# Linear attention and a top-2 expert layer on one core: 32-row gathers issued one at a time over two layers' loops, and a reordered start

## The chip, the cores and the metric

One core of a Trainium2 chip runs the whole kernel. The metric is device time in microseconds. The kernel before took 741.69 us (median of 3 runs, 741.14 to 741.85).

## The reference, cut to what matters

Inputs are q, k, v of shape (4, 8, 768, 64), a decay lam per head, gate and noise weights (512 x 8), noise (3072 x 8), and expert weights w1 (8, 512, 1024) and w2 (8, 1024, 512).

```python
for b in range(nb):                                   # linear attention, a state per head
    intra = einsum('bhij,bhjd->bhid', einsum('bhic,bhjc->bhij', qb, kb) * Dmask, vb)
    inter = einsum('bhid,bhde->bhie', qb * lam_pow, kv_state)
    kv_state = lam_block * kv_state + einsum('bhsd,bhse->bhde', kb * rev_pow, vb)
x = attention output as (3072 tokens, 512)
noisy = x @ w_gate + log1p(exp(x @ w_noise)) * noise  # the two best experts of a token
out[t] = sum over its two experts of weight * (relu(x[t] @ w1[e]) @ w2[e])
```

Dmask, lam_pow and rev_pow are powers of lam. Everything is float32.

## The kernel before, in words

**Attention.** Each of the 12 steps u takes 256 tokens (chunks of 128) of one batch, three steps to a batch. `trans_k` and `trans_q` (L315, L327) transpose k and q on TensorE into PSUM banks `pS` (four of them, taken in turn by `bank()`), evacuated by ScalarE (VectorE for step 0); `trans_q` also lets VectorE write `qTs`, q scaled by `QS`. `scores` (L353) multiplies q by k, and VectorE applies the mask `Mk` into `at`. `kdecay` (L344) scales k on GpSimd into `kd`, of which there is one buffer. `kv` (L401) multiplies kd by v, and `state` (L414) lets VectorE add that to the state. `intra` and `inter` (L381, L376) accumulate the output in the banks `pO` and `pKV`, `evac_o` copies it out, and a step later `store_x`, `products` and `logits` store x and form the gate logits.

**The masks.** VectorE builds the powers of lam by doubling in `pp2`. SyncE (SP) stores them to the DRAM tile `powd` (L203) and loads `at` (L206) and `QS` (L210) from it. VectorE turns `at` round into `Mk` (`make_mask`, L216). All loads of q, k, v, weights and gate weights `wgn` (L667) go through SP's queue in program order. Here `wgn` comes after the loads of step 2.

**The order.** The schedule is written out by hand: each engine works in program order, and waits follow from data and buffers. Before the loop: `trans_k(0)`, `trans_q(0)`, `scores(0)`, `kdecay(0)`, `kv(0)`, `state(0)`, `inter(0, 1)`. The loop of step t (L951) does, for u = t + 1, `trans_k(u)`, `trans_q(u)`, `kv(u)`, `state(u)`, `kdecay(t + 2)`, then `intra(t)`, `inter(t, 0)`, then `scores(u)` and the logits of t - 1. Routing (VectorE) is spread over the steps by `advance`.

**Experts.** For each expert e there is `gemm1` (16 calls, L857: two parts of at most 4 and 3 token tiles by 8 blocks f) and then `gemm2`, one call for each of 6 or 7 token tiles (L893), a tile's result going by VectorE (L919) into one of two `ot` buffers. GpSimd scatters `ot` to the output (`scatter_out`, L926) and fetches what the output held before (`gather_prev`, L891). Beside tile t of `gemm2(e)`, `trans_rows(e + 1, j)` (L829) transposes a tile of gathered rows of the next expert (VectorE, ScalarE), and `gather_rows(e + 2, j)` (L814) refills its buffer `xg`. For e >= 2 a tile is gathered as up to four pieces of 32 columns' width each (L819, an indirect DMA on GpSimd's queue). In the loop of expert 1 the pieces of expert 2, a tile at a time, stand beside the second part of `gemm1(1)` (L1197 to L1199), behind a small copy (`spacer`, L1195) that waits for that block's `ht`; those of expert 3 stand beside `gemm2(1)`.

Of the kernel before, what the change touches and what calls it, by code (L numbers as in the profile page):

```python
# [31 lines left out]
C = 128  # L32
# [5 lines left out]
E = 8  # L38
# [32 lines left out]
X1 = ((), (0,), (1,), (2,), (3,), (4,), (5, 6))  # L71
WARM = (14, 4, 4)
GB = (0, 8, 16, NCH)
# [52 lines left out]
def kernel(  # L126
# [16 lines left out]
    x_tok = dram.tile([NTOK, XW], FT, name="x_tok")  # L143
    powd = dram.tile([H, 2, 256], FT, name="powd")

# [36 lines left out]

    keep_warm(WARM[0])
    for nm in ("kt", "qt"):
        load(0, nm)
    jp = ac.tile([128, 128], I32, name="jp")
# [3 lines left out]
    pp2 = aw.tile([H, 2, 512], FT, name="kd", bufs=1)[:, :, :256]  # L190
    pw, pr = pp2[:, 0, :], pp2[:, 1, 0:255]
    nc.vector.memset(pp2[:, 1, 255:256], 0.0)
    sq = ac.tile([H, 8], FT, name="sq")
    nc.vector.memset(pw[:, :127], 0.0)
    nc.vector.memset(pw[:, 127:128], 1.0)
    nc.vector.tensor_copy(sq[:, 0:1], lamc)
    for i in range(7):
        n = 1 << i
        nc.vector.tensor_scalar(pw[:, 127 + n:127 + 2 * n], pw[:, 127:127 + n], sq[:, i:i + 1], None, op0=MULT)
        nc.vector.tensor_mul(sq[:, i + 1:i + 2], sq[:, i:i + 1], sq[:, i:i + 1])  # L200
    nc.vector.tensor_copy(pw[:, 255:256], sq[:, 7:8])
    nc.vector.tensor_copy(pr, pw[:, 254::-1][:, :255])
    nc.sync.dma_start(powd, pp2)  # L203
    mrev = aw.tile([128, H, C], FT, name="at")
    for a in range(2):
        nc.sync.dma_start(mrev[a * 64:(a + 1) * 64], sub(powd, 256, [[2, 64], [512, H], [1, C]]))  # L206
    load(0, "vt")
    QS = ac.tile([128, HP, C], FT, name="QS")
    for s in range(2):
        nc.sync.dma_start(QS[s * 64:(s + 1) * 64], sub(powd, 128 + 512 * s, [[0, 64], [1024, HP], [1, C]]))  # L210
    Mk = ac.tile([128, 2, HP, C + 1], FT, name="Mk")
    nc.gpsimd.memset(Mk[:, :, :, 0:1], 0.0)

    def make_mask():
        for s in range(2):
            nc.vector.tensor_copy(Mk[:, s, :, 1:], mrev[:, s:H:2, ::-1])  # L216

    def mask(s, h, c):

        m = Mk[:, s, h, c.start + 1:c.stop + 1]  # L220
        return sub(m, 0, [*m.ap[:2], [-1, 2], m.ap[2]])

    for nm in ("kt", "qt", "vt"):
        load(1, nm)
    wgn = ac.tile([128, DB, 32], FT, name="wgn")
    nc.gpsimd.memset(wgn[:, :, 2 * E:], 0.0)
# [36 lines left out]
    class Arena:  # L263
# [4 lines left out]
        def tile(self, shape, dt, name):  # L268
            n = math.prod(shape[1:])
            if name not in self.at:  # L270
                self.at[name], self.end = (self.end, n), self.end + n
            at, most = self.at[name]
            assert n <= most and self.end <= self.buf.shape[1], (name, self.end)
            __import__("sys").stderr.write(f"AR {self.end} ")
# [38 lines left out]

    def trans_k(u):

        kT[u] = aw.tile([128, HP, 2, C], FT, name="kT", bufs=1)
        flat = KT[u].rearrange("p h x d -> p (h x d)")
        for at, y, r in ((D, 1, slice(0, 128)), (0, 0, half(0)), (2 * D, 0, half(1))):
            p = bank()
# [7 lines left out]
    def trans_q(u, scaled=True):  # L327

        qT[u] = aw.tile([128, HP, 2 * C], FT, name="qT", bufs=1)
        qTs[u] = aw.tile([128, HP, 2 * C], FT, name="qTs")  # L330
        for a in range(2):
            p = bank()
# [34 lines left out]
    def add_out(u, a, hp, s, lhs, rhs):  # L367

        if u not in PO:
            PO[u] = [psum.tile([128, DB, C], FT, name=nm) for nm in ("pO", "pKV")]  # L370
            first[u] = {}
        g = side(s, hp)
        n = first[u][a, g] = first[u].get((a, g), 0) + 1
        nc.tensor.matmul(PO[u][a][half(g), hp, :], lhs, rhs, start=n == 1,  # L374
                         stop=n == (12 if u % NW or a else 8))

# [55 lines left out]
    XC = [ac.tile([128, DB, QW], FT, name=f"xc{i}") for i in range(3)]  # L432
    for x in XC:
        nc.gpsimd.memset(x[:, :, C:], 0.0)
    xturn = itertools.count()
# [211 lines left out]

    trans_k(0)
    trans_q(0, False)
    make_mask()  # L650
    keep_warm(WARM[1])
    scores(0)
    nc.vector.tensor_mul(qTs[0][:, :, C:], qT[0][:, :, C:], QS)
    kdecay(0)
    keep_warm(WARM[2])
    kv(0)
    state(0)
    make_sel()
    kdecay(1)
    load(2, "kt")  # L660
    load(2, "qt")
    load(2, "vt")
    inter(0, 1)
    for s, w in ((0, w_gate), (1, w_noise)):
        for d in range(2):
            for h in range(2):
                nc.sync.dma_start(wgn[h * 64:(h + 1) * 64, d::2, s * E:(s + 1) * E],  # L667
                                  sub(w, (d * 128 + (h ^ d) * 64) * E, [[E, 64], [256 * E, DB // 2], [1, E]]))

# [132 lines left out]
    def load_rec(e, queue=nc.sync):  # L802
# [7 lines left out]
        if e >= TURNED:  # L810
# [3 lines left out]
            RECQ[e] = r  # L814

    def gather_rows(e, t, rows=NTOK):
        if e >= TURNED:
            for g in range(size(e, t) // 32):
                nc.gpsimd.indirect_dma_start(  # L819
                    out=XG[t][:, g * QW:(g + 1) * QW], out_offset=None,  # L820
                    in_=x_tok.rearrange("t (q w) -> (t q) w", w=QW),
                    in_offset=bass.IndirectOffsetOnAxis(ap=RECQ[e][:, t, g:g + 1], axis=0),
                    bounds_check=4 * NTOK - 1, oob_is_err=False)
            return
# [123 lines left out]
    def early(b):  # L948

        return [(b, 2 * i, 2, x) for i, x in enumerate(HB[:4 if not b else 2])]  # L950

    got = []
    for t in range(NST):
        u = t + 1
        if u < NST:
            trans_k(u)
        load(t + 3, "kt")
        if u < NST:
            trans_q(u)
        load(t + 3, "qt")  # L960
        if u < NST:
            kv(u)
            state(u)
            kdecay(t + 2)
            if REC and not got:
                for j in range(PARTS0[0]):
                    gather_rows(0, j, GB[1] * C)
                got.append(t)
            advance(FILLS)
        else:  # L970
# [209 lines left out]
    for e in range(1, E):  # L1180
        if e == E - 1:
            n_over = nc.values_load(ntot[0:1, 0:1], min_val=0, max_val=MAXOV)
        if e == 1:
            prepare(2)
        for i, (t0, n) in enumerate(parts(e)):
            for f in range(FB):
# [17 lines left out]
        for t in range(tiles(e)):  # L1204
# [3 lines left out]
            if e + 1 < E:  # L1208
# [83 lines left out]
```

## Time and profile before

| | |
|---|---|
| median of 3 runs | 741.69 us |
| profiled execution | 743.33 us, span 741.5 us |
| TensorE (PE) busy | 706.8 us (95%) |
| VectorE (DVE) | 400.7 us (54%) |
| GpSimd (POOL) | 352.4 us (48%) |
| ScalarE (ACT) | 223.1 us (30%) |
| mean granted TensorE clock | 0.981 |

The profiled execution is one run; its span is from the first to the last instruction. Times in the rows are microseconds from the start of that span unless marked ns. Attention runs to about 145 us, expert 0 to 232 us, and experts 1 to 7 follow.

### The profile page before, as it was taken

The numbers are of one execution on the slowest core, as the hardware profiler recorded it, in microseconds if no ns is written. First come the engines' busy times: TensorE is split into PE (matmuls) and PEld (weight loads), VectorE is DVE, ScalarE is ACT, GpSimd is POOL, SyncE is SP. The second block draws the span as 40 slices with busy tenths as digits, with TensorE's granted clock in tenths as the row PEclk, the third lists the DMA queues.
The fourth block names the chain that finished last, engine by engine and source line by source line (L and its number), as shares of the span: only waits on it lengthen the run. The fifth ranks groups of instructions, "written<-read, shape, count | busy, mean of one in ns | idle before, by whom it ended". The sixth has DMA issues, their size and how long they took to land.

```text
span 741.5 us, 15923 instructions
## 1 busy us (share of the span) xinstructions
PE 706.8 (95%) x6014; PEld 606.1 (82%) x6014; DVE 400.7 (54%) x1053; ACT 223.1 (30%) x381; POOL 352.4 (48%) x503
## 2 busy tenths in 40 slices
PE   6999899999999996879999999999999999999994
PEld 4887788889898895678889887988898898889883
DVE  5645788879456543573457255626552763465210
ACT  0354456451133321132214221422142242214100
POOL 2312163214353488775378547845763776221221
PEclk9899999999999999889999999999999999999998
DMA  7899896681546624445245534634362546230211
GB/s 172 179 270 240 235 231 181 223 308 48 160 141 162 188 50 118 135 128 138 76 166 145 132 101 136 163 91 128 119 157 84 156 147 163 62 136 27 64 43 37
DMA packets 95608, 104.59 MB, mean 141 GB/s; under 512 B 42130, under 2 KB 68260, under 8 KB 95528
## 3 DMA queue, kind: packets, MB, share of 16 engines
q1 hardware_dynamic: 82232, 66.57, 33.9%
q0 software_dynamic: 13296, 36.97, 16.3%
q8 instruction: 49, 0.80, 0.4%
q14 instruction: 31, 0.25, 0.1%
HBM read 78.54 MB, written 26.13 MB: 141 GB/s over the span
## 4 chain that ended last, share of the span: by engine, by line
PE 82%; issue 6%; DMA 4%; DVE 3%; POOL 2%; ACT 1%; SPq 0%; POOLq 0%; DVEq 0%; ACTq 0%
PE pS L869 36%; PE pKV L907 14%; PE pO L907 13%; PE pS L362 3%; PE pO L374 2%; PE pS L321 2%; PE pKV L374 2%; PE pS L442 2%; DMA out_dram<-ot,rec 2%; PE pO L912 1%; PE pS L409 1%; PE pS L334 1%; POOL xg L819 1%; DMA QS<-powd 1%; PE pR L428 1%
## 5 line engine op out<-in xcount | busy, mean ns | idle before, releaser
L869 PE MATMUL pS<-xth,w1h 128*128 128x512 f32 (+3 forms) x544 | 182.5, 335 | 4.6 <-DVE ht L879 4.6
L819 POOL DMA_INDIRECT xg<-x_tok,recq x147 | 160.8, 1094 | 51.0 <-issue 26.6
L869 PE MATMUL pS<-xtl,w1h 128*128 128x512 f32 (+3 forms) x544 | 181.5, 334 | 0.0
L869 PE MATMUL pS<-xth,w1l 128*128 128x512 f32 (+3 forms) x544 | 181.5, 334 | 0.0
L879 DVE SCALAR_TENSOR_TENSOR ht<-pS,ht 128x256 fp32r<-128x256 f32 (+3 forms) x176 | 75.9, 456 | 123.8 <-ACT ht L875 121.5
L907 PE MATMUL pKV<-w2h,ht 128*128 128x512 f32 x384 | 123.9, 393 | 6.2 <-DVE ot L919 6.2
L907 PE MATMUL pO<-w2h,ht 128*128 128x512 f32 x384 | 122.5, 390 | 0.4 <-DVE ot L919 0.4
L875 ACT ACTIVATE ht<-pS 128x512 fp32r<-128x512 f32 (+3 forms) x136 | 65.2, 483 | 173.4 <-PE pS L869 168.2
L869 PEld LDWEIGHTS pS<-xth,w1h 128*128 128x128 f32 x544 | 103.7, 191 | 14.1 <-ACT ht L875 4.0
L869 PEld LDWEIGHTS pS<-xtl,w1h 128*128 128x128 f32 x544 | 103.8, 191 | 8.9
L869 PEld LDWEIGHTS pS<-xth,w1l 128*128 128x128 f32 x544 | 103.6, 190 | 8.8
L926 POOL DMA_INDIRECT out_dram<-ot,rec x46 | 54.9, 1192 | 95.1 <-DVE ot L919 84.1
L907 PEld LDWEIGHTS pKV<-w2h,ht 128*128 128x128 f32 x384 | 72.9, 190 | 21.8 <-DVE ot L919 6.7
L907 PEld LDWEIGHTS pO<-w2h,ht 128*128 128x128 f32 x384 | 72.1, 188 | 15.6 <-DVE ot L919 0.8
L840 ACT ACTIVATE xth<-turned 128x512 fp32r<-128x512 f32 (+1 forms) x39 | 23.7, 607 | 180.7 <-DVE turned L838 180.7
L907 PE MATMUL pKV<-w2l,ht 128*128 128x512 f32 x192 | 75.5, 393 | 0.0
L907 PE MATMUL pO<-w2l,ht 128*128 128x512 f32 x192 | 74.8, 390 | 0.0
L350 POOL TENSOR_TENSOR kd<-kt,Mk 128x512 f32<-128x512 f32 x24 | 24.8, 1055 | 87.9 <-PE pR L409 54.0
L891 POOL DMA_INDIRECT pv<-out_dram,rec x46 | 47.1, 1023 | 30.2 <-issue 22.3
L919 DVE SCALAR_TENSOR_TENSOR ot<-pKV,wr,pv 128x512 f32<-128x512 f32 x21 | 15.8, 751 | 54.6 <-PE pKV L907 41.5
L907 PEld LDWEIGHTS pKV<-w2l,ht 128*128 128x128 f32 x192 | 36.5, 190 | 7.5
L790 DVE TENSOR_TENSOR w2l<-wst,w2h 128x1024 fp32r<-128x1024 f32 (+1 forms) x33 | 39.1, 1188 | 5.6 <-ACT w2h L789 5.6
(221 smaller groups left out, 960.8 us busy)
## 6 DMA issues: line engine op xcount, KB each, us to landing
wst<-in_moe_w_dram SPq DMA_DIRECT2D x36, 512.0 KB, 4.0
wst<-in_moe_w_dram SPq DMA_DIRECT2D x96, 128.0 KB, 3.5
x_tok<-xc SPq DMA_DIRECT2D x24, 272.0 KB, 4.5
kt<-in_k_dram SPq DMA_DIRECT2D x12, 512.0 KB, 6.5
qt<-in_q_dram SPq DMA_DIRECT2D x24, 256.0 KB, 6.4
vt<-in_v_dram SPq DMA_DIRECT2D x12, 512.0 KB, 6.3
out_dram<-zero SPq DMA_DIRECT2D x24, 256.0 KB, 3.6
xg<-x_tok,recq POOLq DMA_INDIRECT x147
```

The lines of the kernel that those rows point to most:

```text
L350: nc.gpsimd.tensor_mul(kd[:, :, s], kt[:, :, s], mask(s, slice(0, HP), slice(C - 1, C)).to_broadcast([128, HP, 2, D]))
L362: nc.tensor.matmul(ps[s][half(a), h, x, :], kT[u][half(s), 2 * r + h, x ^ s, half(a)], qT[u][half(s), 2 * r + h, a * C:(a + 1) * C], start ...
L374: nc.tensor.matmul(PO[u][a][half(g), hp, :], lhs, rhs, start=n == 1, stop=n == (12 if u % NW or a else 8))
L790: nc.vector.tensor_tensor(lo[:, r], st[:, r], hi[:, r].bitcast(FT), op=SUB)
L819: nc.gpsimd.indirect_dma_start(out=XG[t][:, g * QW:(g + 1) * QW], out_offset=None, in_=x_tok.rearrange("t (q w) -> (t q) w", w=QW), in_off ...
L840: nc.scalar.activation(hi, raw, AF.Copy)
L869: nc.tensor.matmul(p, W1[a][d][:, fs], xt(b, cs)[:, d], start=(d == 0 and i == 0), stop=(d == DB - 1 and i == 2))
L875: nc.scalar.activation(ht(e, 0, f, cs), p, AF.Relu)
L879: nc.vector.scalar_tensor_tensor(ht(e, 1, f, c), p[:, r], 0.0, ht(e, 0, f, c).bitcast(FT), op0=OP.max, op1=SUB)
L891: nc.gpsimd.indirect_dma_start(out=PV[t][:size(e, t), :], out_offset=None, in_=out, in_offset=bass.IndirectOffsetOnAxis(ap=REC[e, t], axis=0),
L907: nc.tensor.matmul(p, ht(e, a, f, cs), W2[b][f // 2][:, f % 2, :], start=(i == 0), stop=(i == len(terms) - 1))
L926: st = nc.gpsimd.indirect_dma_start(out=out, out_offset=bass.IndirectOffsetOnAxis(ap=REC[e, t], axis=0), in_=o, in_offset=None, bounds_che ...
```

## The change

Eight edits, in the order of the program:

- The loads of `wgn` stand right behind those of k and q of step 0, and k of step 1 comes before v of step 0. In the prologue the loads of step 2's q and step 1's v come first, then step 2's k and v.
- The powers of lam are built in one direction, without the squares and the reversed copy. ScalarE's queue stores them, and loads `Mk` directly in four transfers. The mask is read with stride -1. `make_mask` is gone.
- `QS` comes from four TensorE products of a 0/1 matrix `one` with the powers, copied out by ScalarE.
- 14 warming products become 12; two further groups of 4 become one of 2.
- `trans_k(1)` and `trans_q(1)` stand before `kv(0)`, in the banks pO, pKV and pL; `intra(0)`, `inter(0, 0)` and `evac_o(0)` move ahead of the loop, and one half of step 0's inter term is formed late and added to the copied output.
- In the loop `trans_q(u)` stands behind `kv(u)`, `state(u)` and `kdecay`.
- The memsets of `xc` move down the program.
- `gather_rows` of an expert from 2 on puts its pieces into a list. One piece is issued after each `gemm1` call and up to two after each `trans_rows` beside `gemm2`. Expert 2's whole list is there at the start of expert 1.

```diff
+    for nm in ("kt", "qt"): load(0, nm)          # unchanged, and then
+    wgn = ac.tile([128, DB, 32], FT, name="wgn")
+    ... (the eight loads of w_gate and w_noise, as at L667)
+    load(1, "kt")
-        nc.vector.tensor_scalar(pw[:, 127 + n:127 + 2 * n], pw[:, 127:127 + n], sq[:, i:i + 1], None, op0=MULT)
-        nc.vector.tensor_mul(sq[:, i + 1:i + 2], sq[:, i:i + 1], sq[:, i:i + 1])
+        nc.vector.tensor_scalar(pw[:, 128 - 2 * n:128 - n], pw[:, 128 - n:128], pw[:, 128 - n:129 - n], None, op0=MULT)
+    nc.scalar.dma_start(powd, pw)
+    for s in range(2):
+        for a in range(2):
+            nc.scalar.dma_start(Mk[a * 64:(a + 1) * 64, s, :, :C], sub(powd, 256 * s + 1, [[2, 64], [512, HP], [1, C]]))
+    def make_scale():
+        p = psum.tile([128, HP, C], FT, name="pR")
+        for hp in range(HP):
+            nc.tensor.matmul(p[:, hp, :], one[:, 1, hp, :], pw[:, :C], start=True, stop=True)
+        nc.scalar.activation(QS, p[:, :, ::-1], AF.Copy)
+    load(0, "vt")
+    load(1, "qt")
+    keep_warm(WARM[0])
+    make_scale()
...
     trans_k(0)
-    trans_q(0, False)
-    make_mask()
+    trans_q(0)
+    load(2, "qt")
+    load(1, "vt")
+    scores(0)
+    kdecay(0)
+    load(2, "kt")
+    load(2, "vt")
+    trans_k(1, ("pO", "pKV", "pL"))
+    trans_q(1, ("pO", "pKV"))
     keep_warm(WARM[1])
-    scores(0)
-    nc.vector.tensor_mul(qTs[0][:, :, C:], qT[0][:, :, C:], QS)
-    kdecay(0)
-    keep_warm(WARM[2])
     kv(0)
+    kdecay(1)
+    intra(0)
     state(0)
+    for a in range(2):
+        cs = slice(a * C, (a + 1) * C)
+        nc.vector.tensor_mul(qTs[1][:, :, cs], qT[1][:, :, cs], QS)
+    inter(0, 0)
+    evac_o(0)
+    scores(1)
+    for hp in range(HP):
+        nc.tensor.matmul(PO[0][0][half(side(0, hp)), hp, :], SA[0, 1][half(0), hp, :], qTs[0][half(0), hp, C:],
+                         start=True, stop=True)
+    for g in range(2):
+        xo = XO[0][half(g), 1, g::2, :]
+        nc.vector.tensor_add(xo, xo, PO[0][0][half(g), g::2, :])
+    kv(1)
+    state(1)
     make_sel()
-    kdecay(1)
-    inter(0, 1)
+    inter(1, 1)
...
+    pieces = []
+    def gather_pieces(n):
+        for e, t, g in pieces[:n]:
+            nc.gpsimd.indirect_dma_start(... one piece, as at L819 ...)
+        del pieces[:n]
     def gather_rows(e, t, rows=NTOK):
         if e >= TURNED:
-            for g in range(size(e, t) // 32):
-                nc.gpsimd.indirect_dma_start(...)
+            pieces.extend((e, t, g) for g in range(size(e, t) // 32))
             return
...
         if e == 1:
             prepare(2)
+            for t in tile_order(2):
+                gather_rows(2, t)
...
-                if (t0 == 0 or e == 1) and f < tiles(e):
+                if t0 == 0 and f < tiles(e):
                     nc.gpsimd.tensor_copy(spacer, ht(e, 0, f, columns(e, t0, n))[0:1, 0:1].bitcast(FT))
-                    if t0 == 0:
-                        gather_prev(e, f)
-                    else:
-                        gather_rows(2, tile_order(2)[f])
+                    gather_prev(e, f)
+                gather_pieces(1)
...
                 for j in nxt[t:t + 1]:
                     trans_rows(e + 1, j)
+                    gather_pieces(2)
                     if e + 2 < E and j < tiles(e + 2):
                         gather_rows(e + 2, j)
```

## Rows read from the trace of the kernel before

**Rows 1.** The page: busy time by engine; granted clock in 40 slices.

```profile
PE 706.8 (95%) x6014; PEld 606.1 (82%) x6014; DVE 400.7 (54%) x1053; ACT 223.1 (30%) x381; POOL 352.4 (48%) x503
PEclk9899999999999999889999999999999999999998
```

**Rows 2.** Windows: length; busy of PE, PEld, DVE, ACT, POOL; PEclk; DMA share; GB/s.

```profile
268.98:356.57 87.59, 75.92 (x354) 64.15 (x353) 40.27 (x93) 19.86 (x32) 64.03 (x75) 0.92 0.42 120
392.89:463.62 70.73, 70.73 (x354) 59.85 (x354) 36.78 (x80) 20.14 (x32) 44.15 (x53) 1.00 0.47 129
sum 333.00, PE 333.00 PEld 281.63 DVE 169.26 ACT 92.64 POOL 193.52; mean PE 66.60 PEld 56.33 DVE 33.85 ACT 18.53 POOL 38.70
```

**Rows 3.** Timeline, 274 to 297 us: start, length, instruction, [idle before <- releaser].

```profile
274.49 0.75 DVE L919 SCALAR_TENSOR_TENSOR ot<-pKV,wr,pv 128x512 f32<-128x512 f32 x1 [3.88 <-PE pKV L907]
278.88 0.80 DVE L843 SCALAR_TENSOR_TENSOR w<-rank,xg 32x7 f32<-32x7 f32 x4
296.19 0.75 DVE L919 SCALAR_TENSOR_TENSOR ot<-pKV,wr,pv 128x512 f32<-128x512 f32 x1 [11.15 <-DMA out_dram<-ot,rec]
297.00 0.79 PE L907 MATMUL pKV<-w2h,ht 128*128 128x512 f32 x1 [6.23 <-DVE ot L919]
```

**Rows 4.** Timeline of GpSimd, 253 to 300 us.

```profile
253.70 0.98 POOL L891 DMA_INDIRECT pv<-out_dram,rec  x1 [0.57 <-issue]
...
258.12 1.04 POOL L819 DMA_INDIRECT xg<-x_tok,recq  x1 [0.62 <-issue]
259.46 1.00 POOL L819 DMA_INDIRECT xg<-x_tok,recq  x1 [0.30 <-issue]
...
293.33 1.01 POOL L926 DMA_INDIRECT out_dram<-ot,rec  x1 [0.23 <-issue]
...
297.29 2.07 POOL L819 DMA_INDIRECT xg<-x_tok,recq  x1 [0.30 <-DMA xg<-x_tok,recq]
```

**Rows 5.** Groups by line, GpSimd, 330 to 705 us: count, busy, mean ns, idle before.

```profile
L819 POOL DMA_INDIRECT xg<-x_tok,recq x102 | 111.9, 1097 | 37.9 <-issue 18.9 <-DVE w L843 11.0 <-DVE turned L838 1.8
L891 POOL DMA_INDIRECT pv<-out_dram,rec x39 | 39.9, 1022 | 24.4 <-issue 19.6 <-DMA out_dram<-ot,rec 4.8
```

**Rows 6.** The chain of waits, in order of time.

```profile
27.58 1.17 issue
...
30.88 1.46 PE pS L321 x12
...
356.57 5.44 PE pO L907 x24
...
389.21 3.68 PE pO L912 x16
```

**Rows 7.** Timeline of SP and the engines, 7 to 34 us.

```profile
8.46 0.63 SPq L206 DMA_DIRECT2D at<-powd  x1
11.10 0.61 SPq L165 DMA_DIRECT2D kt<-in_k_dram  x1
11.76 4.62 SPq L161 DMA_DIRECT2D qt<-in_q_dram  x2
13.23 0.77 DVE L216 COPY Mk<-at 128x512 f32<-128x512 f32 x2 [2.44 <-DMA at<-powd]
15.92 0.31 PE L409 MATMUL pS<-vt,kd 64*64 64x64 f32 x2 [2.35 <-POOL kd L350]
21.86 1.91 PE L334 MATMUL pS<-identf,qt 128*128 128x128 f32 x8
23.70 0.37 PE L409 MATMUL pS<-vt,kd 64*64 64x64 f32 x2
24.75 3.79 SPq L667 DMA_DIRECT2D wgn<-in_moe_w_gate_dram  x4
28.57 3.49 SPq L667 DMA_DIRECT2D wgn<-in_moe_w_noise_dram  x4
32.18 0.53 SPq L165 DMA_DIRECT2D kt<-in_k_dram  x1
```

**Rows 8.** Windows of 2 us at the start, columns as in rows 2.

```profile
20.00:22.00 2.00, 2.00 (x11) 2.00 (x10) 1.93 (x3) 1.19 (x2) 2.00 (x4) 0.50 0.97 264
30.00:32.00 2.00, 2.00 (x41) 1.83 (x33) 1.95 (x4) 0.44 (x1) 0.00 (x0) 1.00 0.08 4
```

**Rows 9.** Tile qt: DMA to landing. Then TensorE's waits, 24 to 165 us: total, times, longest.

```profile
DMA to landing us min/median/max: 6.1/6.1/6.1
PE pKV L374 <- issue: 2.2, 1, 2.2
PE pS L362 <- issue: 2.0, 3, 1.2
PE pS L409 <- issue: 1.5, 2, 0.8
PE pS L869 <- DVE ht L879: 0.8, 1, 0.8
PE pS L321 <- DVE at L365: 0.8, 1, 0.8
```

More of the change, by code (lines that the diff above doesn't have):

```diff
@@ L71 @@
 X1 = ((), (0,), (1,), (2,), (3,), (4,), (5, 6))
-WARM = (14, 4, 4)
+WARM = (12, 2)
 GB = (0, 8, 16, NCH)
@@ L143 @@
     x_tok = dram.tile([NTOK, XW], FT, name="x_tok")
-    powd = dram.tile([H, 2, 256], FT, name="powd")
+    powd = dram.tile([H, 256], FT, name="powd")
     lamc = ac.tile([H, 1], FT, name="lamc")
@@ L181, in side @@
         return s ^ (hp & 1)
-    keep_warm(WARM[0])
     for nm in ("kt", "qt"):
         load(0, nm)
+    wgn = ac.tile([128, DB, 32], FT, name="wgn")
+    for s, w in ((0, w_gate), (1, w_noise)):
+        for d in range(2):
+            for h in range(2):
+                nc.sync.dma_start(wgn[h * 64:(h + 1) * 64, d::2, s * E:(s + 1) * E],
+                                  sub(w, (d * 128 + (h ^ d) * 64) * E, [[E, 64], [256 * E, DB // 2], [1, E]]))
+    load(1, "kt")
     jp = ac.tile([128, 128], I32, name="jp")
@@ L189 @@
     nc.vector.tensor_scalar(identf, jp, 0.0, None, op0=OP.is_equal)
[L190 to L196, printed above, removed]
+    one = aw.tile([H, 2, HP, C], FT, name="xo")
+    nc.gpsimd.iota(one[:, 0].bitcast(I32).rearrange("p h (s i) -> p h s i", s=2), pattern=[[2, HP], [1, 2], [0, C // 2]],
+                   base=0, channel_multiplier=-1)
@@ L197 @@
+    pw = aw.tile([H, 2, 512], FT, name="kd", bufs=1)[:, 0, :256]
+    nc.vector.memset(pw[:, 129:], 0.0)
+    nc.vector.memset(pw[:, 128:129], 1.0)
+    nc.vector.tensor_scalar(one[:, 1], one[:, 0].bitcast(I32), 0.0, None, op0=OP.is_equal)
+    nc.vector.tensor_copy(pw[:, 127:128], lamc)
     for i in range(7):
         n = 1 << i
-        nc.vector.tensor_scalar(pw[:, 127 + n:127 + 2 * n], pw[:, 127:127 + n], sq[:, i:i + 1], None, op0=MULT)
-        nc.vector.tensor_mul(sq[:, i + 1:i + 2], sq[:, i:i + 1], sq[:, i:i + 1])
@@ L201 @@
[L201 to L206, printed above, removed]
-    load(0, "vt")
-    QS = ac.tile([128, HP, C], FT, name="QS")
-    for s in range(2):
-        nc.sync.dma_start(QS[s * 64:(s + 1) * 64], sub(powd, 128 + 512 * s, [[0, 64], [1024, HP], [1, C]]))
@@ L211 @@
[L211 to L225, printed above, removed]
+        nc.vector.tensor_scalar(pw[:, 128 - 2 * n:128 - n], pw[:, 128 - n:128], pw[:, 128 - n:129 - n], None, op0=MULT)
@@ new lines @@
+    nc.scalar.dma_start(powd, pw)
+    Mk = ac.tile([128, 2, HP, C + 1], FT, name="Mk")
+    nc.gpsimd.memset(Mk[:, :, :, C:], 0.0)
+    for s in range(2):
+        for a in range(2):
+            nc.scalar.dma_start(Mk[a * 64:(a + 1) * 64, s, :, :C], sub(powd, 256 * s + 1, [[2, 64], [512, HP], [1, C]]))
+    QS = ac.tile([128, HP, C], FT, name="QS")
+    def make_scale():
[3 more added lines that the diff above has]
+        nc.scalar.activation(QS, p[:, :, ::-1], AF.Copy)
@@ L226, with mask @@
+    def mask(s, h, c):
+        m = Mk[:, s, h, C - c.stop:C - c.start]
+        return sub(m, c.stop - c.start - 1, [*m.ap[:2], [1, 2], [-1, c.stop - c.start]])
+    load(0, "vt")
+    load(1, "qt")
+    keep_warm(WARM[0])
+    make_scale()
     nc.gpsimd.memset(wgn[:, :, 2 * E:], 0.0)
@@ L273, in tile @@
             assert n <= most and self.end <= self.buf.shape[1], (name, self.end)
-            __import__("sys").stderr.write(f"AR {self.end} ")
             v = self.buf[:, at:at + n]
@@ L312, in half, with trans_k @@
         return slice(i * 64, (i + 1) * 64)
-    def trans_k(u):
+    def trans_k(u, banks=()):
+        banks = iter(banks)
         kT[u] = aw.tile([128, HP, 2, C], FT, name="kT", bufs=1)
@@ L318, in trans_k @@
         for at, y, r in ((D, 1, slice(0, 128)), (0, 0, half(0)), (2 * D, 0, half(1))):
-            p = bank()
+            nm = next(banks, None)
+            p = psum.tile([128, HP, C], FT, name=nm) if nm else bank()
             for hp in range(HP):
@@ L325, in trans_k, with trans_q @@
                 nc.vector.tensor_copy(kT[u][r, :, y, :], p[r])
-    def trans_q(u, scaled=True):
+    def trans_q(u, banks=()):
+        scaled = not banks
+        banks = iter(banks)
         qT[u] = aw.tile([128, HP, 2 * C], FT, name="qT", bufs=1)
@@ L331, in trans_q @@
         for a in range(2):
-            p = bank()
+            nm = next(banks, None)
+            p = psum.tile([128, HP, C], FT, name=nm) if nm else bank()
             for hp in range(HP):
@@ L374, in add_out @@
         nc.tensor.matmul(PO[u][a][half(g), hp, :], lhs, rhs, start=n == 1,
-                         stop=n == (12 if u % NW or a else 8))
+                         stop=n == (8 if not (u % NW or a) else 12 if u else 10))
     def inter(u, x):
@@ L432 @@
     XC = [ac.tile([128, DB, QW], FT, name=f"xc{i}") for i in range(3)]
-    for x in XC:
-        nc.gpsimd.memset(x[:, :, C:], 0.0)
     xturn = itertools.count()
@@ L648 @@
     trans_k(0)
-    trans_q(0, False)
-    make_mask()
+    trans_q(0)
[7 more added lines that the diff above has]
+    trans_q(1, ("pO", "pKV"))
     keep_warm(WARM[1])
-    scores(0)
-    nc.vector.tensor_mul(qTs[0][:, :, C:], qT[0][:, :, C:], QS)
-    kdecay(0)
-    keep_warm(WARM[2])
     kv(0)
+    kdecay(1)
+    intra(0)
     state(0)
-    make_sel()
-    kdecay(1)
-    load(2, "kt")
-    load(2, "qt")
-    load(2, "vt")
-    inter(0, 1)
[L664 to L668, printed above, removed]
+    for a in range(2):
[12 more added lines that the diff above has]
+    state(1)
+    make_sel()
+    inter(1, 1)
     def places(b):
@@ L814, in load_rec @@
             RECQ[e] = r
+    pieces = []
+    def gather_pieces(n):
+        for e, t, g in pieces[:n]:
+            nc.gpsimd.indirect_dma_start(
+                out=XG[t][:, g * QW:(g + 1) * QW], out_offset=None,
+                in_=x_tok.rearrange("t (q w) -> (t q) w", w=QW),
+                in_offset=bass.IndirectOffsetOnAxis(ap=RECQ[e][:, t, g:g + 1], axis=0),
+                bounds_check=4 * NTOK - 1, oob_is_err=False)
+        del pieces[:n]
     def gather_rows(e, t, rows=NTOK):
         if e >= TURNED:
-            for g in range(size(e, t) // 32):
[L819 to L823, printed above, removed]
+            pieces.extend((e, t, g) for g in range(size(e, t) // 32))
             return
@@ L833, in trans_rows @@
         if e >= TURNED:
+            assert not any((e, t) == p[:2] for p in pieces), (e, t)
             hi, lo = [xt(i, slice(t * TS, t * TS + n)) for i in range(2)]
@@ L950, in early @@
         return [(b, 2 * i, 2, x) for i, x in enumerate(HB[:4 if not b else 2])]
+    for x in XC:
+        nc.gpsimd.memset(x[:, :, C:], 0.0)
     got = []
@@ L954 @@
         u = t + 1
-        if u < NST:
+        if t and u < NST:
             trans_k(u)
         load(t + 3, "kt")
[L958 to L961, printed above, removed]
+        if not t:
+            kdecay(2)
+        elif u < NST:
             kv(u)
@@ L968 @@
                 got.append(t)
+            trans_q(u)
+        load(t + 3, "qt")
+        if not t:
+            pass
+        elif u < NST:
             advance(FILLS)
@@ L976 @@
             advance(FILLS)
-        intra(t)
+        if t:
+            intra(t)
         load(t + 3, "vt")
-        inter(t, 0)
-        evac_o(t)
-        if u < NST:
+        if t:
+            inter(t, 0)
+            evac_o(t)
+        if t and u < NST:
             if t:
```

## The prediction, made before the changed kernel was run

> **What bounds the kernel now.** I read the page first: TensorE is busy 95% of the span and no other engine more than 54% [rows 1], so what can be won is the time in which TensorE stands still or runs slowly. The clock line beneath has digits under 9 in the second slice and in three of the slices around 300 us and behind it [rows 1]. Those two places are where I looked further; from 333 us to 666 us TensorE is busy 333.00 us of 333 [rows 2], and an edit can win nothing there.
>
> The larger place is the turn from expert 1 to expert 2. Cut at the first product of a layer's gemm2 and at the first one of the next layer's, the windows for expert 1 and for expert 2 hold the same 354 products; one takes 87.59 us and the other 70.73 us [rows 2]. So the turn loses 16.86 us: 87.59 - 75.92 = 11.67 us with TensorE idle, and 75.92 - 70.73 = 5.19 us in which the same products take longer, at a mean granted clock of 0.92 against 1.00 [rows 2].
>
> The timeline says why. TensorE's long gap, 6.23 us before 297.00, ends with VectorE's copy into `ot`, and that had itself waited 11.15 us for the DMA that empties one of the two `ot` buffers [rows 3]. The scatter of the first tile could have been issued when `ot` was written, at 274.49 + 0.75 = 275.24; GpSimd issued it at 293.33 [rows 3, 4], 18.1 us late. In between GpSimd's queue holds pieces of expert 2's gather: the first starts at 258.12, behind all seven gathers of earlier output (the last at 253.70), and they come one per 1.30 to 1.34 us [rows 4]. The pieces were ahead of the scatter in program order, and there were too many of them for the time that was left.
>
> The smaller place is the start. Step 2 begins at 30.88 [rows 6], and before it come late masks (VectorE waits 2.44 us for `at`), products that wait for GpSimd's kd, and SP, which sits from 24.75 to 32.06 on the eight small `wgn` loads before k of step 3 can go out [rows 7]. In 30 to 32 us the DMA engines are 0.08 busy [rows 8]. In 20 to 22 us TensorE is busy throughout but at a granted clock of 0.50, the lower of its two levels [rows 8].
>
> **The gathers.** Expert 2 has 25 pieces. After the change 16 stand beside the 16 calls of gemm1(1), one each, and 9 beside gemm2(1), followed there by the first 5 of expert 3. Per tile of gemm2, GpSimd then has one scatter and two pieces, 3 x 1.31 = 3.9 us against TensorE's 5.44 us [rows 4, 6]: no queue builds up if none is there at the start. Is one there? In gemm1 the pieces take 16 x 1.30 = 20.8 us, the seven gathers of earlier output 7 x 1.53 = 10.7 us (1.02 busy [rows 5], some 0.5 for the copy ahead and its gaps, as the 0.57 in rows 4), in all 31.5 us. One gemm1 with its 16 calls lasts 70.73 - 6 x 5.44 - 3.68 = 34.41 us [rows 2, 6]. So the queue fits with 2.9 us to spare, and the first scatter goes out near its time. The pieces arrive in time too: tile 4's are 1 to 4 of the list, tile 3's 22 to 25, issued by the fifth tile of gemm2 and transposed beside the seventh.
>
> What is late next in that stretch is VectorE: its work beside one tile of gemm2(1) runs from 274.49 to 279.68 [rows 3], 5.2 us of 5.44. That just fits, with 0.2 us to spare per tile, and it is tighter than in later layers, since the overflow table's steps stand there only in expert 1. I take 1.0 us of the loss as left; the bounds are nothing left and half of it, 8.4. **Term 1: 16.86 - 1.0 = 15.9 us won**, between 8.4 and 16.9.
>
> In the layers behind, the pieces only move (16 of 25 into gemm1). TensorE has no idle time there, so nothing is won; the cover is the 2.9 us to spare per gemm1.
>
> [...] Pieces move from gemm2 to a place where VectorE works on weights. In the trace a piece takes 1.00 to 1.04 us, and 2.07 us at 297.29, where VectorE's subtraction for `w1l` was running [rows 4]; the mean of 102 is 1.097 [rows 5]. [...]
>
> **The start.** Masks: four mask loads of one size stand in ScalarE's queue for two in SP's, behind a store that goes out about when it did. At 0.63 us an issue [rows 7] the last goes out at about 9.6 instead of 8.46, and I let the masks land as late as now, at 13.2. The turned copy of 0.77 us [rows 7] is gone. This wins 0.4 to 0.8 us for scores and kd, but it does not decide: `kv(0)` now stands on TensorE behind `trans_q(1)`, which waits for q of step 1.
>
> SP issues k and q of step 0 until 3.6, then the eight `wgn` loads: at 0.91 each as now (3.79 + 3.49 over 8) to 10.9, or at 0.61 as its plain loads [rows 7] to 8.5. Then k (0.61), v (0.62), and q's two: 1.25 as two other transfers take, or 4.62 as now [rows 7]. So q goes out by 11.0 to 16.7; with 6.1 us to land [rows 9] it is there between 17.1 and 22.8. I take 18, near the early end, since the DMA engines had room then. `trans_q(1)` ends 0.9 later, 18.9 (1.9 us later at the low clock of rows 7 and 8).
>
> From there to step 2 TensorE does what it did from 23.70 to 30.88 [rows 6, 7], 7.2 us with a stall of 1.17 in it [rows 6], and also `kv(0)` (1.2), two warming products and four small ones (0.5): 8.9 us. Before `inter(1, 1)` it waits for VectorE: behind scores(1) come a mask product, two additions and four state steps, some 2.2 us against 1.0 of `kv(1)`, so 1.2 us. Step 2 then starts at 18.9 + 8.9 + 1.2 = 29.0 instead of 30.88. **Term 2: 1.9 us won**; the ends are 17.1 + 0.9 + 8.9 - 1.2 = 25.7 (5.2 won, no stall and no wait) and 22.8 + 1.9 + 8.9 + 1.2 = 34.8 (3.9 lost).
>
> **The loop.** SP no longer spends 7.3 us on `wgn` at 25 to 32 us; k of step 3 goes out up to 7 us earlier. Between 24 and 165 us TensorE idles 5.7 us on "issue" and 1.6 us behind VectorE [rows 9]. State steps put ahead of the q products let VectorE work while ScalarE copies q. I take **term 3: 1.0 us won**, between 4 won (over half of the 7.3) and 3 lost (as many more such stalls).
>
> **Sum.** 15.9 + 1.9 + 1.0 = 18.8. From the profiled execution's 743.33 (span 741.5, and 1.8 around it): 724.5. That execution stands 1.64 above the median of the runs, 741.69, so the forecast for the median is 722.9.
>
> **Rivals.**
>
> A. *The start turns against it.* TensorE is held behind q of step 1, which lands as late as now. For: q's two issues took 4.62 us [rows 7], the DMA engines were 0.97 busy in 20 to 22 us [rows 8]. Against: the `wgn` loads leave those engines nearly idle [rows 8]. Term 2 is -3.9 and term 3 is 0: 741.69 - 15.9 + 3.9 = 729.7.
>
> B. *VectorE takes over the turn.* 5.2 us of 5.44 leave no room for one delayed step. Half of the hole stays: 741.69 - 8.4 - 2.9 = 730.4. Against: the two PSUM banks and two `ot` buffers let TensorE run a tile ahead.
>
> C. *The pieces fill gemm1: slower.* If each piece beside gemm1 is held up as the one at 297.29, GpSimd's queue overruns into gemm2 in every layer from 1 to 6 and scatters go out late again. Two `ot` buffers cover two tiles, 10.9 us, and 2.9 us are to spare: it decides from (10.9 + 2.9)/16 = 0.86 us more per piece, 2.16 us. At 1.3 us more (2.6 each) the overrun is 20.8 - 13.8 = 7 us per layer, 42 us in six: 741.69 - 18.8 + 42 = 765. Against: the mean of 102 is 1.097 [rows 5].
>
> D. *The hole isn't the pieces' doing,* but the DMA's own slowness: then only the start moves and the time stays within 739 to 743. Against: the scatter's 18.1 us late issue [rows 3, 4].
>
> **How the numbers follow.** Forecast 0.68, its own range 716 to 728 (term 2's and 3's good and middling ends, term 1 from 14 to 16.9). A 0.12, B 0.11, C 0.05, D 0.04. The predicted time is the forecast's, 722.9. The range 714 to 732 reaches A and B and leaves out C, D and the tails. A difference below 0.2% (1.5 us) can't be told from no change here. Faster: forecast, A, B and a little of D, 0.92; same, most of D, 0.03; slower, C, 0.05.
>
> **What would show it.** The window of 354 products from gemm2(1) on falls from 87.59 to 71 to 73 us at a granted clock near 1.00. The first scatter of expert 1 is issued within 2 us of its `ot`. The wait of `ot` for the out_dram DMA is gone from that stretch. Pieces beside gemm1 take 1.0 to 1.2 us. Step 2's first transposition starts at 26 to 31 us, with `trans_q(1)` at about 18, ahead of `kv(0)`. I am wrong if TensorE idles at the ends of gemm2 in later layers (C), if VectorE's copies to `ot` start late with the scatters on time (B), or if step 2 starts behind 31 us (A).

## The result, and the profile after

The changed kernel takes **722.97 us** (median of 4 runs, 722.62 to 724.83) where the kernel before took 741.41 beside it (740.69 to 741.85): ratio 0.9757, interval 0.9739 to 0.9776. Beside experiments 1 to 11 the kernel before took 789 to 815 us instead of 741, with TensorE standing on "issue" in the gemms as well, and a ratio given there is taken over its shorter executions alone, so those runs are compared only with each other, and by stretches of their traces.

The profiled executions are 743.33 and 722.93, 20.40 us apart. Cut at the same places of the program in both traces, this is where they come from:

| Stretch | before | after | won | predicted |
|---|---|---|---|---|
| start to step 2 | 30.88 | 32.78 | -1.90 | +1.9 |
| step 2 to gemm2(1) | 238.10 | 232.24 | +5.86 | +1.0 |
| gemm2(1) to gemm2(2) | 87.59 | 70.86 | +16.73 | +15.9 |
| behind it, to the end of the span | 384.93 | 385.22 | -0.29 | 0 |

The page after (busy time by engine, granted clock, and the queue of instruction blocks: packets, MB), beside [rows 1]:

```profile
PE 703.4 (98%) x6014; PEld 603.5 (84%) x6014; DVE 398.4 (55%) x1044; ACT 223.5 (31%) x382; POOL 357.4 (50%) x497
PEclk9999999999999999999999999999999999999998
q8 instruction: 49, 0.80, 0.5%
```

TensorE is 98% busy, and the digits under 9 around 300 us are gone.

**The turn.** Windows of the changed kernel, columns as in [rows 2]: expert 1 to expert 2, and one later layer.

```profile
265.02:335.88 70.86, 70.86 (x353) 60.73 (x353) 40.10 (x93) 19.88 (x32) 48.34 (x57) 1.00 0.45 133
371.40:442.13 70.73, 70.73 (x354) 59.83 (x353) 36.77 (x81) 20.14 (x32) 48.98 (x56) 1.00 0.48 131
```

The turn that took 87.59 now costs 0.13 us more than a later layer, and TensorE is busy throughout at full clock. GpSimd's timeline, as in [rows 4], shows why, and its group by line answers to [rows 5]:

```profile
254.04 0.98 POOL L916 DMA_INDIRECT pv<-out_dram,rec  x1 [0.16 <-issue]
255.33 1.01 POOL L838 DMA_INDIRECT xg<-x_tok,recq  x1 [0.30 <-issue]
...
267.25 1.00 POOL L838 DMA_INDIRECT xg<-x_tok,recq  x1 [0.30 <-issue]
268.24 0.09 POOL L950 MEMSET spacer<- 1x1 f32 x1
271.55 1.01 POOL L951 DMA_INDIRECT out_dram<-ot,rec  x1 [3.22 <-DVE ot L944]
272.87 1.04 POOL L838 DMA_INDIRECT xg<-x_tok,recq  x1 [0.30 <-issue]
```
```profile
L838 POOL DMA_INDIRECT xg<-x_tok,recq x147 | 161.4, 1098 | 45.4 <-issue 41.8 <-ACT ht L900 2.1 <-ACT w2h L806 0.6
```

GpSimd is done with the 16 pieces at 268.25, which is 3.2 us behind the first product of gemm2(1), and still waits 3.22 us for `ot` before the first scatter, at 271.55; before, that scatter went out 18.1 us late. A piece takes 1.098 us in the mean, as it did.

**The start.** The chain of waits up to step 2, in order of time (as in [rows 6]):

```profile
9.77 5.42 DMA kt<-in_k_dram
15.21 7.24 DMA Mk<-powd
22.59 1.06 POOL kd L359
...
32.78 1.46 PE pS L327 x12
```

Timeline of the engines at the start, as in [rows 7], and two of TensorE's waits there:

```profile
2.41 1.76 DVE L206 TENSOR_SCALAR kd<-kd 8x1 f32<-8x1 f32 x7
...
3.66 3.46 SPq L189 DMA_DIRECT2D wgn<-in_moe_w_gate_dram  x4
...
6.36 2.07 PE L219 MATMUL pR<-kd,xo 8*128 8x128 f32 x8
...
7.16 2.56 SPq L189 DMA_DIRECT2D wgn<-in_moe_w_noise_dram  x4
...
8.22 0.73 ACTq L207 DMA_DIRECT2D powd<-kd  x1
...
9.96 5.84 ACTq L212 DMA_DIRECT2D Mk<-powd  x4
...
11.03 8.70 SPq L161 DMA_DIRECT2D qt<-in_q_dram  x4
...
15.84 0.60 ACT L220 ACTIVATE QS<-pR 128x512 f32<-128x512 f32 x1 [13.62 <-DMA Mk<-powd]
...
21.90 0.63 PE L343 MATMUL pKV<-identf,qt 128*128 128x128 f32 x4
...
23.69 0.27 PE L418 MATMUL pS<-vt,kd 64*64 64x64 f32 x1 [0.58 <-POOL kd L359]
```
```profile
PE pS L371 <- DVE qTs L350: 2.0, 1, 2.0
PE pS L418 <- POOL kd L359: 0.6, 1, 0.6
```

VectorE has the powers at 4.17; their store goes out on ScalarE's queue only at 8.22, the four mask loads hold that queue till 15.8 (one such load takes 0.63 [rows 7]), and the masks land at 22.45. Before, they were there at 13.2 [rows 7]. ScalarE copies `QS` out only behind those loads, at 15.84, and TensorE waits 2.0 us for `qTs`, which is made with it.

q of step 1 is late too. SP issues it behind the eight gate-weight loads, from 11.03 to 15.12 (the first two of the four in the row), and its second half lands at 21.77, where it landed at 21.35 before. `trans_q(1)` starts on that half at 21.90 and ends at 22.53; behind it TensorE waits 0.58 us more, for kd, which needs the masks.

**The loop.** TensorE's waits from 24 to 165 us (total, times, longest), as in [rows 9], and one window of the kernel before and of the one after, from step 2 to gemm2(0):

```profile
PE pKV L383 <- DVE S L430: 1.2, 1, 1.2
PE pS L894 <- DVE ht L904: 0.8, 1, 0.8
PE pS L343 <- issue: 0.6, 1, 0.6
PE pR L418 <- issue: 0.3, 1, 0.3
```
```profile
30.88:163.98 133.10, 126.85 (x2753) 111.57 (x2754) 94.02 (x312) 69.97 (x132) 35.21 (x70) 0.99 0.87 236
```
```profile
32.78:160.04 127.26, 125.73 (x2753) 109.86 (x2754) 94.14 (x319) 69.75 (x132) 34.41 (x71) 1.00 0.84 240
```

Idle time falls from 133.10 - 126.85 = 6.25 to 1.53 us. "Issue" alone falls from 5.7 [rows 9] to 0.9.

### The profile page after: what moved, and what is told of

It is laid out like the page before. It is cut to its first block, busy times and chain, and to the rows that moved or that the text cites. A ratio compares the mean times of both kernels' runs of the same rounds, so it can differ in the third digit from the quotient of the medians.

```text
span 721.1 us, 15837 instructions
## 1 busy us (share of the span) xinstructions
PE 703.4 (98%) x6014; PEld 603.5 (84%) x6014; DVE 398.4 (55%) x1044; ACT 223.5 (31%) x382; POOL 357.4 (50%) x497
## 4 chain that ended last, share of the span: by engine, by line
PE 87%; issue 5%; DVE 3%; DMA 2%; SPq 1%; POOL 1%; ACT 0%; POOLq 0%; DVEq 0%; ACTq 0%
PE pS L894 37%; PE pKV L932 16%; PE pO L932 16%; PE pO L383 3%; PE pS L371 2%; PE pS L327 2%; PE pS L449 2%; PE pO L937 2%; PE pS L418 1%; PE pS L343 1%; PE pKV L937 1%; DMA Mk<-powd 1%; PE pKV L383 1%; PE pR L437 1%; PE pS L873 1%
## 5 line engine op out<-in xcount | busy, mean ns | idle before, releaser
L951 POOL DMA_INDIRECT out_dram<-ot,rec x46 | 60.6, 1318 | 119.7 <-DVE ot L944 112.5
L374 DVE TENSOR_TENSOR at<-pS,Mk 128x512 f32<-128x512 f32 x48 | 29.8, 681 | 22.9 <-PE pS L371 18.1
```

The costliest lines, as they stand in the source:

```text
L374: nc.vector.tensor_mul(at[:, s], ps[s], mask(s, slice(2 * r, 2 * r + 2), slice(0, C)))
L951: st = nc.gpsimd.indirect_dma_start(out=out, out_offset=bass.IndirectOffsetOnAxis(ap=REC[e, t], axis=0), in_=o, in_offset=None, bounds_che ...
```

## The experiments

**1 and 2. The gathers alone** (kernel before, nothing but the list of pieces changed), twice.

```diff
-            for g in range(size(e, t) // 32): nc.gpsimd.indirect_dma_start(...)
+            pieces.extend((e, t, g) for g in range(size(e, t) // 32))
...
+                gather_pieces(1)      # behind each gemm1 call
+                    gather_pieces(2)  # beside each tile of gemm2
```

> The kernel before with the gathers' list alone, start and loop as they were. Theory 1 (the pieces of expert 2 stood ahead of the scatters and that is the whole of the turn's loss): the stretch of 354 products from gemm2(1) on takes 71 us instead of 87.59, and the time falls by 16 to 17 us, to about 725. Rival (the turn is mended only because the changed start and loop come to it with other work done): the stretch stays above 78 us and the time above 732.

> The kernel before with the gathers' list alone, once more, on another run of the chip. Theory 1 (the turn from expert 1 to 2 is the list's doing and nothing else of the change touches it): the stretch from gemm2(1)'s first product to gemm2(2)'s takes 70.7 to 71.5 instead of 87.59, and the time is 16 to 17 below before, 724.5 to 725.5, ratio 0.977 to 0.979; then start and loop together are worth 2 of the whole 18.4. Rival (the start and loop of the change help the turn too, by where the chip stands when it gets there): ratio 0.982 or more.

736.0 us (ratio 0.9197, interval 0.9128 to 0.9267) and 738.35 (0.9305, 0.9196 to 0.9414), both with the kernel before at some 806, so the expected times can't be read off; the stretch can. In the second run gemm2(1) to gemm2(2) takes what it takes in the changed kernel:

```profile
278.06:348.89 70.83, 70.83 (x353) 60.73 (x353) 40.19 (x93) 19.76 (x32) 44.06 (x52) 1.00 0.45 128
```

(73.56 in the first run.) The turn is the list's doing; no other part of the change is needed for it.

**3. The changed kernel with the old gathers.**

> The changed kernel with the gathers as before, so start and loop alone. If the parts add up: 722.97 + 16.7 = 739.7, some 1 to 2 us under the kernel before; if the turn's loss had shrunk through the earlier arrival alone, under 735.

801.99 us, ratio 0.9892 (0.9836 to 0.9947): nearly all of the gain is gone. The same stretch has the hole again, larger on this chip (the execution in the trace took 807.32 us):

```profile
267.34:368.28 100.94, 85.65 (x353) 67.00 (x354) 42.16 (x102) 20.83 (x34) 59.89 (x75) 0.85 0.36 103
```

That stretch is not all of it. The next four layers, gemm2 to gemm2, take 80.4 to 84.2 us each in this trace, where the changed kernel's take 65.9 to 73.2 in experiment 9; why the old gathers cost time there as well is not settled.

**4. The loop order alone** (kernel before).

```diff
         if u < NST:
-            trans_q(u)
-        load(t + 3, "qt")
-        if u < NST:
             kv(u)
             state(u)
...
+            trans_q(u)
+        load(t + 3, "qt")
+        if u < NST:
             advance(FILLS)
```

> The kernel before with the loop's order alone: trans_q(u) behind kv(u), state(u) and kdecay; start and gathers as they were. Theory 2 (the order spreads the dense small products, so that TensorE's instruction blocks come in time): TensorE's idle time on issue between 24 and 165 us falls from 5.7 us to under 2, and the time by 3 to 5 us, to about 737. Rival a (the gate weights' loads at 25 to 32 us are the cause of the loop's stalls, through SP and the DMA engines): within 1 us of 741.4, issue 4 to 6 us. Rival b (a block's boundary falls elsewhere by chance): also here a change of the stalls' places, but their sum between 3 and 7 us.

808.35 us, ratio 1.0016 (0.9957 to 1.0075): no change that can be seen. "Issue" in 24 to 165 us falls to 2.8, but gemm2(0) begins at 162.37, where it begins at 162.06 in experiment 1 with the old order. Step 2 begins at 32.16 there, and from it to gemm2(0) the trace takes 130.39 us (TensorE idle 3.87). The kernel with the old order takes 131.04 (6.04 idle) in experiment 1 and 129.50 (4.04 idle) in experiment 2. These two are one kernel, so traces differ by as much as the order could bring here, and this one run can't show it.

**5. The changed kernel with the old loop order** (experiment 4's edit undone).

> The changed kernel with the loop's old order (trans_q(u) ahead of kv(u)). Theory 2: the stalls on issue come back, 3 to 6 us between 34 and 165 us, and the time rises by 3 to 5 us to about 727. Rival a (the gate weights' place): within 1 us of 723, as they are still loaded first. Rival b (boundaries by chance): anything between.

734.58 us (ratio 0.9149, 0.9089 to 0.9209; the changed kernel was not timed on that chip, but on another, where the kernel before takes as long, it took 734.22 in experiment 9, so by time the old order costs nothing that can be seen). The window from step 2 to gemm2(0), and beside it those of experiments 3 and 9, which have the new order:

```profile
33.93:165.28 131.35, 125.67 (x2754) 110.34 (x2754) 94.64 (x319) 69.69 (x132) 36.15 (x71) 1.00 0.84 233
```
```profile
34.33:161.81 127.48, 126.61 (x2753) 111.10 (x2754) 94.51 (x318) 69.72 (x132) 34.91 (x71) 0.99 0.82 238
32.76:162.20 129.44, 126.23 (x2754) 110.23 (x2754) 95.22 (x319) 69.46 (x132) 35.41 (x71) 1.00 0.83 235
```

With the changed start, the nine traces that have the new order take 127.05 to 129.44 us for this window, with 0.9 to 3.2 us of idle TensorE, and the one with the old order takes 131.35, with 5.68. So the order is worth some 1.9 to 4.3 us there, by a single trace of the old one. Three of its waits in 24 to 165 us:

```profile
PE pS L371 <- issue: 3.2, 4, 1.4
PE pR L418 <- issue: 1.8, 2, 1.1
...
PE pS L418 <- issue: 0.6, 1, 0.6
```

**What "issue" is.** For each such stop in attention I counted TensorE's instructions (weight loads, products and the waits among them) from the start of the trace, and set the resume beside the last block of 16 KB on the queue named "instruction". Worked out from the two traces:

```
kernel  instruction  block lands  TensorE stops  resumes  resume - landing
before      705         27.50        27.58        28.75        1.26
before     1473         43.84        44.70        45.37        1.53
before     1985         55.20        55.84        56.69        1.48
before     2241         60.70        61.84        62.09        1.38
before     2753         72.03        72.94        73.54        1.51
before     3009         79.81        78.92        81.07        1.26
after       705         28.17        29.40        29.67        1.50
after      1473         45.35        46.31        46.89        1.55
```

Every number is 193 + 256 k, the landings follow the same count, and in no kernel here does TensorE pass such a number earlier than 1.25 us after its block has landed. In experiment 6, with 12 instructions fewer ahead, the stop is at 705 again, which is then another product of the program. So these stops are TensorE waiting for its own instructions. The "issue" stops in the gemms beside experiments 1 to 11 (6.8 us in experiment 9's trace, 39.4 in experiment 3's) stand at other numbers; they are something else, and stay unexplained. The time from passing one such number to the start of the next block's transfer is 2.2 to 2.5 us in the mean in the four traces with the old order (before and experiments 1, 2, 5) and 1.4 to 1.8 in the ten with the new one. The Trainium skill, page "Runtime: NRT & Kernel Launch", section "Instruction fetch mechanics", has engines take instructions in 16 KiB blocks of 256 and calls the cost of a block's boundary "mostly hidden"; the size and the count agree with the trace, the cost does so only in part: 4.5 us of the kernel before's 133.10 stand at five such boundaries.

**6. Less warming**, so that make_scale's 2.07 us, which my sum left out, fall into time that TensorE has to spare.

```diff
-WARM = (12, 2)
+WARM = (6, 2)
```

> The changed kernel with 6 instead of 12 warming products ahead of the first transposition, so that make_scale's 2.07 us of TensorE, which my sum left out, stand inside the time in which TensorE has nothing to do. Theory 1 (the 2.07 us count only where nothing later waits; step 2 is held by the masks): trans_k(0) begins about 2 us earlier than 8.36, the masks still land at 22 or later, step 2 begins within 0.5 us of 32.78, and the time is the changed kernel's, 722 to 724, ratio 0.974 to 0.977. Rival (make_scale is on the path): step 2 at 30.7, time 720.9, ratio 0.972.

732.78 us (ratio 0.9234, 0.9123 to 0.9345). trans_k(0) begins at 6.44 instead of 8.36, and step 2 at 33.08, as late as ever; the chain goes through the masks:

```profile
4.44 2.07 PE L219 MATMUL pR<-kd,xo 8*128 8x128 f32 x8
```
```profile
15.77 6.98 DMA Mk<-powd
22.89 1.06 POOL kd L359
```

make_scale is covered. What holds the masks?

**7 and 8. The gate weights over GpSimd's queue**, without and with experiment 6's edit. In the compiled program the transfers that SP and ScalarE issue take eight completion counters in turn, and each waits until the one eight places ahead has landed. From the changed kernel's list (place, engine, tile, place that it waits for):

```
13  ScalarE  powd  <- 5 (a wgn load)
17  ScalarE  Mk    <- 9 (a wgn load)
18  ScalarE  Mk    <- 10 (a wgn load)
20  ScalarE  Mk    <- 12 (k of step 1)
```

```diff
-                nc.sync.dma_start(wgn[h * 64:(h + 1) * 64, d::2, s * E:(s + 1) * E],
+                nc.gpsimd.dma_start(wgn[h * 64:(h + 1) * 64, d::2, s * E:(s + 1) * E],
```

The loads also move down the program, behind `load(1, "qt")`; what is left on SP's queue keeps its order. By the trace of the changed kernel the store goes out at 8.22, 0.08 us after the load at place 5 has landed, and the last mask load at 15.21, 0.02 us after k of step 1 has.

> The changed kernel with one thing else: the eight gate-weight loads go out over GpSimd's queue and no longer over SP's. Same bytes, about the same moment. Theory 1 (order, not traffic: in the compiled program the transfers of SP and ScalarE share eight completion counters taken in turn, and a transfer waits until the one eight places ahead has landed; so the powers' store stands behind a gate-weight load and the last mask load behind k of step 1): the store goes out within 1 us of the last power, at about 4.5 instead of 8.22, the masks land by 16 instead of 22.45, and step 2 begins at 28 to 30 instead of 32.78. The time is 3 to 5 us below the changed kernel's, 718 to 720, ratio to before 0.969 to 0.972. Theory 2 (the transfers are slow because the DMA engines are full at the start): masks land at 20 or later, step 2 begins at 32 to 33, the time stays at 722 to 724, ratio 0.974 to 0.977.

> Both of the two edits above. If the masks are what holds the start and make_scale stands next, the two add up: masks by 16, trans_k(0) at about 6.4, step 2 at 26 to 28.5, time 716 to 719, ratio 0.966 to 0.970, and this beats both kernels. If traffic holds the masks: step 2 at 31 to 33, time 721 to 724. If q of step 1 is what holds step 2 once the masks are early (my prediction's own view), step 2 begins 9 to 11 us behind the landing of q of step 1, whatever the warming.

732.3 us (ratio 0.9215, 0.9124 to 0.9305) and 731.55 (0.9207, 0.9086 to 0.9328; five executions of 726.92 to 733.32 and one of 1410.95, which stays unexplained): by time alone not to be told from experiment 6. By the trace, theory 1: the store goes out at 4.31, as VectorE ends; step 2 begins at 27.77 and 27.94, 5.3 and 5.1 us before experiment 6's. The masks land at 17.4 to 17.6, not by 16: loads of Mk still take 7.1 us. Warming again changes nothing. q of step 1 doesn't come last here: TensorE waits 0.6 to 0.9 us for it, and 1.1 to 1.3 for kd behind it. That doesn't clear it in the changed kernel. With the eight loads gone, SP issues q from 6.25 instead of 11.03, and in experiment 7 it lands at 16.02 instead of 21.77. So the edit brings masks and q forward together, and neither was moved alone.

**9 and 10. The changed kernel, and experiment 7's, side by side.**

> The changed kernel unaltered, so that the two versions sent with it stand beside it on the same chip. Both theories: step 2 begins at 32.5 to 33.5, its masks land at 22 to 23; 723 us (ratio 0.974 to 0.977) where the kernel before takes 741, and 732 to 734 where it takes some 806.

> The changed kernel with the gate weights over GpSimd's queue, once more, now beside the changed kernel itself. Theory 1 (the 5 us that step 2 began earlier in its first run reach the end, since TensorE is busy throughout what follows): step 2 at 27.5 to 28.2 and a time 4 to 6 us below the changed kernel's on this chip. Rival (the 5 us are given back in the loop, where loads of later steps are late instead): step 2 as early, but the time within 1.5 us of the changed kernel's, and the stretch from step 2 to gemm2(1) 4 us longer than its 232.24.

734.22 us (ratio 0.9182, 0.9117 to 0.9246) and 730.94 (0.9135, 0.9066 to 0.9204): 3.3 us apart with intervals that overlap. Step 2 is at 32.76 and at 29.59, later than expected, since TensorE stopped for two instruction blocks (0.88 and 1.68 us at instructions 449 and 705).

**11. qTs(1) by GpSimd as well.**

```diff
-        nc.vector.tensor_mul(qTs[1][:, :, cs], qT[1][:, :, cs], QS)
+        nc.gpsimd.tensor_mul(qTs[1][:, :, cs], qT[1][:, :, cs], QS)  # ahead of kdecay(1)
```

> The kernel of the run ahead of this one, and the two mask products for qTs(1), 2.0 us of VectorE between the state steps of step 0 and the masks of scores(1), moved to GpSimd, which idles there. Theory 1 (VectorE's queue sets step 2 once the masks are early): step 2 at 26.5 to 27.2, 0.6 to 1.3 us below the run ahead of this one. Rival (TensorE's own stall of about 0.9 us in kv(1), which comes behind an instruction block, ends last): step 2 within 0.3 us of that run's and the time the same.

731.42 us (ratio 0.9141, 0.9073 to 0.921), no better, and step 2 at 28.02, between experiment 7's 27.77 and experiment 10's 29.59, so at neither of the expected places. From the chain:

```profile
24.07 1.37 issue
25.45 0.27 PE pR L418
26.43 0.29 DVE S L430
```

The rival's mechanism is there: VectorE begins the masks of scores(1) at 22.76 instead of 23.16 in experiment 7, and TensorE then stands 1.37 us at instruction 705.

**12. Experiment 7's kernel where the kernel before takes 742.**

> The changed kernel with the gate weights over GpSimd's queue, a third time, to see it where the kernel before takes 741. If it is: step 2 at 27.5 to 28.2 and a time of 717 to 719.5, ratio 0.967 to 0.971, against 722.97 for the changed kernel. On a chip like those of the three calls before it: 730 to 733. Rival (the 5 us are lost again where nothing is disturbed): 722 to 724, ratio 0.974 to 0.977. In both cases TensorE's stops in attention that are put down to issue lie at instruction numbers 193 + 256 k of its stream, 1.2 to 1.7 us behind the landing of an instruction block; a stop of that kind at another number would tell against the blocks as their cause.

**719.66 us** (718.55 to 720.41), ratio 0.9697 (0.9677 to 0.9718) to 742.29: it beats both kernels, the changed one by 3.3 us with intervals apart, and lies 0.2 us above what I expected. Its chain up to step 2, and the two ends of the turn:

```profile
4.33 3.97 DMA powd<-kd
8.38 0.65 ACTq L205
...
10.40 6.91 DMA Mk<-powd
17.45 1.06 POOL kd L359
...
24.27 1.23 issue
...
28.13 2.50 PE pS L327 x12
...
260.33 5.46 PE pKV L932 x24
...
331.19 5.44 PE pO L932 x24
```

Step 2 begins 32.78 - 28.13 = 4.65 us earlier than in the changed kernel, gemm2(1) 4.69 and gemm2(2) 4.69: up to there nothing is given back. The masks land at 17.32 and q of step 1 at 15.92. The one "issue" stop of over 0.3 us in attention is at instruction 705, 1.46 us after its block landed.

## Why the prediction was right, and where it was not

The time is within 0.1 us of the forecast, but not by its terms: they sum to 18.8 and the profiled executions stand 20.40 apart. The errors are +0.8, -3.8, +4.9 and -0.3, 1.6 in all, and the 1.64 by which I lowered the forecast, since the profiled execution of before stood above its median, cancels that: the one of after stands on its median. That the time came out so close is luck.

**Term 1 was right**, 15.9 against 16.73, and so was its mechanism: scatters on time and the wait of `ot` gone, as experiments 1 to 3 show. One step beneath it failed without harm. I had the queue done 2.9 us ahead of gemm2, and the pieces end 3.2 us behind its first product: GpSimd's first gather beside gemm1(1) starts at 236.07, 7.2 us behind that gemm1's first product at 228.88, and I counted from the start of gemm1. The cover was one that my sum didn't use, the time until the first `ot` is there. The 1.0 us that I left for VectorE was too much; 0.13 is left.

**Term 2 had the wrong sign.** Two steps of it failed, both by the eight gate-weight loads. The first is "the last goes out at about 9.6 instead of 8.46, and I let the masks land as late as now, at 13.2". I counted issues on ScalarE's queue and took the queue for independent of SP's. It isn't: the store stood 4 us behind a gate-weight load, the last mask load behind k of step 1, and the masks landed at 22.45. The second is q of step 1, which I took to be there at 18, near the early end of its range; it landed at 21.77, and `trans_q(1)` ended at 22.53 instead of 18.9. From there my own 8.9 + 1.2 us give 32.6, and step 2 began at 32.78, so the rest of the working holds.

Masks and q came 0.7 us apart. The masks came last, where I wrote that they do not decide, but by the trace they hold TensorE only 0.58 us beyond `trans_q(1)`. Experiments 7, 8 and 12 show that the eight loads on SP's queue make the start late: with the same bytes over another queue step 2 comes at 28.13. How much of that is the masks' and how much q's is not shown, since the edit moved both. make_scale, uncosted, takes 2.07 us and is covered (experiment 6).

Rival A, the start turning against the change, is thus what happened in the start: q of step 1 landed as late as before (21.77 against 21.35), and the masks, which A did not name, later still.

**Term 3 was too small**: 1.0 against 5.86, beyond its upper bound of 4. 6.25 - 1.53 = 4.7 us of it is TensorE's idle time from step 2 to gemm2(0), of which 3.9 are stops at instruction blocks (4.5 behind step 2 before, 0.58 after). I had the row, 5.7 us of "issue" [rows 9], and gave its stops no cause of their own. Experiment 5 gives some 1.9 to 4.3 us to the loop order, given the changed start; experiment 4 can't show what it is worth without. Some 1.1 us of the 5.86, a shorter busy time of TensorE, stays unexplained.

Rivals B and C didn't come: no `ot` is late in the turn, and pieces beside gemm1 take 1.0 to 1.2 us. D falls with experiments 1 to 3. One reading was loose, and nothing hangs on it: of the three clock slices under 9 "around 300 us and behind it" two stand at the turn, and the third is the last slice of the span [rows 1].

## What to carry to other kernels

Cost a DMA that moves to another queue by everything that it can wait for, not by the issues ahead of it on that queue: here a tiny store stood 4 us behind a load of another engine. A scatter or store that frees a buffer belongs ahead of bulk gathers in program order, and the gathers fit where their issue times, counted from the start of the first, end before the first scatter is due. Idle time on "issue" is worth a look at instruction numbers: stops at a fixed spacing were TensorE waiting for code here.

## What the runs showed that I had not expected

- Completion counters tie SP's and ScalarE's queues together: the store waited from 4.17 to 8.22 us and goes out at 4.31 to 4.33 once eight unrelated loads leave SP's queue.
- TensorE resumes 1.25 us or more behind the landing of its next 256 instructions, and 4.5 us of attention hung on it. That the block's transfer starts later with the old order because step loads are then under way is a guess that I did not try.
- A start that is 4.65 us earlier is worth 4.37 in the profiled execution and 3.3 in the medians; up to gemm2(2) all of it is kept.
